# One sum and one product a chunk on GpSimd in 20 chunks, and newly ordered queues, in a gated linear recurrence followed by a gated convolution

## The chip, the cores and the metric

The kernel runs on one core of one Trainium2 chip. The metric is the time of one execution in microseconds (us); lower is better. The kernel before takes 281.59 us, the median of three runs.

## What is computed

The inputs x, r_gate and i_gate are float32 tensors of 4 sequences x 6336 steps x 256 channels. The reference, cut to what matters:

```python
# stage 1: gated linear recurrence along the sequence
a_base = 1 / (1 + exp(-a_param))                      # one number a channel
log_a  = 8 * sigmoid(r_gate) * log(clip(a_base, 1e-6, 1 - 1e-6))
a_t    = exp(log_a)
x_gated = sqrt(maximum(1 - a_t * a_t, 1e-6)) * sigmoid(i_gate) * x
h = 0
for t in range(S):                                    # S = 6336, per sequence
    h = a_t[:, t] * h + x_gated[:, t]
    y[:, t] = h
# stage 2, on y
gate = sigmoid(causal_conv(y, conv_w))                # 5 taps, channel by channel
out  = (gate * (y @ w_val)) @ w_out                   # both 256 x 256
```

## The kernel before

The four sequences are laid end to end: 25344 rows of 256 channels. They are cut into windows of 512 rows (window 49 has 256), and windows into 27 chunks: chunks 0, 1, 25 and 26 are one window each, chunks 2 to 24 are two, so that chunk c holds the windows 2c-2 and 2c-1. A window of r, i and x is loaded with rows on the partitions; the recurrence needs channels on the partitions, and TensorE transposes in between. The 256 channels are two halves, h = 0 and 1. For output, window 49 is cut in two parts of 128 rows, 49 and 50.

Nothing is scheduled by the compiler. A string, `ORDER`, lists some 960 words; each word emits one step, and each engine, and the one queue that starts all large DMAs (SyncE, SP), works through its own steps in the order of the string. What follows the @ in a word are PSUM banks. A word is a step name, the chunk or window, and sometimes the half. With the lines of the kernel before, the steps are:

- SP: `lr`, `li`, `lx` load a window of r, i, x (line 292) into rings of four windows (`rring`, `iring`, `xring`); `st` stores a window from `oring` (line 562); `s_wl` loads parts of the weights. A load waits until the earlier content of its place has been read, and everything behind it in the queue waits too.
- ACT (ScalarE): `ta`, `tb` tanh of r and i of a chunk (lines 310, 313); `ex` the decay a, by Exp, into `aring` (373; from chunk 2 to 23 two chunks at once); `rt` the square root of a batch of chunks (406, between two table loads at 578); `tg` tanh of the convolution of a window (518); `ca` copies a window's result to `oring` (551); `sa` squares the decay (389).
- POOL (GpSimd): `sq` squares the decay of a chunk's half into `ering` (381); `pp` adds 1 to the tanh of i of one window in place in `tbring` (320); `up` multiplies that by x into `uring` (332); `s_wcast` casts the weights.
- DVE (VectorE): `rd` a square root by arithmetic for chunk 0 (419 to 427, eight operations); `uv` the product of x in windows 0, 2, 4, 8 and 9, where TensorE has brought x to PSUM (346); `xg` times the root (452, and 456 from chunk 24 on); `sc` the scan along time (499); `gv` gate times value (531); `cd` copies a window's result to `oring` (549).
- PE (TensorE): `tr` (357), `xp` (337), `nt` (441) and `xt` (466) transposes, `cv` the convolution (511), `vl` the product with w_val (526), `ou` the product with w_out (541).

A chunk therefore runs: loads, `ta`, `tr`, `ex`, squares, `rt`, `nt`, then (with `tb`, `pp`, `up` beside it) `xg`, `xt`, `sc`; then by windows `cv`, `tg`, `vl`, `gv`, `ou`, `ca` or `cd`, `st`. The roots are taken in batches: chunk 0 by `rd.0.0`; chunk 1, and chunks 2 and 3, by `rt.1.0` and `rt.2.0`; then four chunks at a time by `rt.3` to `rt.7`, in two pieces each; chunk 24 by `rt.8.0`, chunks 25 and 26 by `rt.8.1`. From chunk 24 on `xg` follows the transpose, and the scan reads `uring` instead of PSUM.

Of the kernel before, what the change touches and what calls it, by code (L numbers as in the profile page):

```python
# [9 lines left out]
P = 128  # L10
CONV_K = 5
# [15 lines left out]
NU = 10  # L27
# [8 lines left out]
NOSB = 4  # L36
GROUPS = [[0], [1], [2, 3], [4, 5], [6, 7], [8, 9], [10, 11], [12, 13], [14, 15], [16, 17], [18, 19], [20, 21], [22,
# [7 lines left out]
s_ident s_small s_kt s_diag lr.1 lr.0 lr.2 lr.3 li.0 ta.1 lr.5 tr.1.1@3 ta.0 tr.1.0@1 ex.1.0 lr.4 tr.0.1@2 li.1 ex.0.1  # L45
tr.0.0@1 lx.0 ex.0.0 sq.0.1 ta.2 sq.0.0 sq.1.0 rd.0.0 tb.0 lr.6 lr.7 ex.1.1 li.3 li.2 sq.1.1 ta.3 lx.1 s_wl.0 lx.3 tb.1
tr.2.1@2,3 li.5 pp.1 ex.2.1 tr.2.0@0,1 s_wl.3 ex.2.0 lx.2 sq.2.1 lr.8 ta.4 sq.3.0 s_wl.1 tb.2 lr.9 xp.0@0,1 sq.3.1 li.4
uv.0 s_wl.2 nt.0@6 sq.2.0 xg.0 li.7 rt.1.0 li.6 xt.0.0@2 up.1 sc.0.0 rt.2.0 nt.1@0 lx.4 xt.0.1@3 sc.0.1 xp.2@6,7 pp.3
lx.5 xg.1 lr.11 uv.2 up.3 lr.10 nt.2@0,1 xt.1.0@2 ta.5 cv.0@4,5 sc.1.0 s_wcast xg.2 tb.3 lr.12 tr.4.1@2,3 lr.13
xt.1.1@6 xt.2.1@0 sc.1.1 tg.0 li.9 sc.2.1 li.8 ex.4.1 vl.0@4,5 xt.2.0@1 tr.4.0@6,7 tb.4 gv.0 sq.5.1 cv.1@2,3 sc.2.0  # L50
ex.4.0 li.11 pp.5 lx.7 xp.4@4,5 lx.6 pp.6 uv.4 ta.6 pp.7 nt.3@6,7 up.5 ou.0.0@0,1 ta.7 lr.14 cv.3@4,5 cd.0.0 li.10
sq.5.0 lx.9 xg.3 tg.3 cv.2@0,1 lr.15 tg.1 lx.8 st.0 vl.1@6,7 sq.4.1 tg.2 xt.3.1@4 gv.1 tb.5 tr.6.0@0,1 sc.3.1 up.7
tr.6.1@6,7 ex.6.0 vl.2@2,3 up.6 lx.11 gv.2 li.12 ou.1.0@4,5 ex.6.1 lr.17 cd.1.0 xt.3.0@2 lr.16 sq.4.0 lx.10 sc.3.0
li.13 tb.6 ou.2.0@6,7 sq.7.0 vl.3@0,1 ta.8 li.15 cv.4@4,5 gv.3 sq.6.1 cd.2.0 tg.4 lr.18 ou.3.0@2,3 cd.3.0 sq.7.1
xp.8@0,1 lx.12 uv.8 rt.3.0 li.14 vl.4@2,3 st.1 sq.6.0 gv.4 lr.19 xp.9@6,7 uv.9 pp.11 lx.13 ou.4.0@2,3 rt.3.1 pp.10
cd.4.0 st.2 nt.4@6,7 up.10 xg.4 nt.5@0,1 xg.5 xt.4.0@4 up.11 lx.14 sc.4.0 xt.5.0@3 nt.6@6,7 tb.7 xt.4.1@2 sc.4.1
# [553 lines left out]
```

## Time and profile before

| | before |
|---|---|
| runs | 281.40, 281.59, 281.83 us; median 281.59 |
| span of the profiled execution | 279.6 us from the first to the last instruction; the median of the runs is 2.0 us longer |
| busy: ACT, DVE, PE, POOL | 267.0, 258.2, 243.8, 233.0 us (96, 92, 87, 83% of the span) |
| granted TensorE clock, mean | 0.993 |
| DMA | 104.75 MB, mean 375 GB/s; 405 to 420 GB/s in most slices before 240 us |

The page is of one execution. Its second part shows how the engines' busy share moves through the span, in 40 slices of 7 us. In the lists of groups a duration is the mean of one instruction; on ACT, DVE and POOL an instruction starts about 0.05 to 0.15 us before the one ahead of it ends, so that from start to start is a little less than the duration. "Before" a group stands the idle time of its engine and what ended it.

### The profile page before, as it was taken

How to read it: one execution, taken by the hardware profiler on the slowest of the kernel's cores; microseconds unless marked ns; L12 is line 12 of the kernel's file. 1: busy time of each engine (PE TensorE's matmuls, PEld its weight loads, DVE VectorE, ACT ScalarE, POOL GpSimd, SP SyncE). 2: the span in 40 equal slices, each digit the busy share in tenths (PEclk: the TensorE clock that was granted, in tenths of full speed). 3: DMA queues.
4: the chain of work that ended last, by engine and by line, in shares of the span. 5: the costliest groups of instructions: out<-in, count | busy, mean ns of one | idle time of the engine just before them, and what ended most of it. 6: DMA issues, size and time to landing. Idle time of an engine off the chain costs nothing. (4 is left out here: it accounts for less than half of the span.)

```text
span 279.6 us, 6233 instructions
## 1 busy us (share of the span) xinstructions
PE 243.8 (87%) x2493; PEld 164.9 (59%) x2493; DVE 258.2 (92%) x221; ACT 267.0 (96%) x187; POOL 233.0 (83%) x152
## 2 busy tenths in 40 slices
PE   2368999898799779999889999899999899999994
PEld 2143566456647466874566575666675756856563
DVE  5587797899999999899999999999999999999992
ACT  5999999999999999999999999999999999999754
POOL 1569679997999998999999999999999977984200
PEclk9998899999999999999999999999999999999999
DMA  7999999999999999999999999999999999742765
GB/s 275 411 405 385 388 409 409 413 409 409 419 408 417 415 414 416 413 416 409 420 413 341 415 420 414 414 411 420 416 363 407 420 378 400 286 176 92 283 263 194
DMA packets 29563, 104.75 MB, mean 375 GB/s; under 512 B 3287, under 2 KB 4062, under 8 KB 29534
## 3 DMA queue, kind: packets, MB, share of 16 engines
q1 hardware_dynamic: 29520, 104.35, 94.4%
q8 instruction: 19, 0.31, 0.4%
q14 instruction: 10, 0.08, 0.1%
q10 hardware_dynamic: 14, 0.01, 0.0%
HBM read 78.39 MB, written 25.95 MB: 373 GB/s over the span
## 5 line engine op out<-in xcount | busy, mean ns | idle before, releaser
L381 POOL TENSOR_TENSOR ering<-aring 128x1024 f32<-128x1024 f32 (+1 forms) x51 | 90.7, 1799 | 13.8 <-ACT aring L373 13.7
L332 POOL TENSOR_TENSOR uring<-tbring,xring 128x1024 bf16<-128x1024 bf16 (+1 forms) x45 | 95.5, 2139 | 3.2 <-DMA xring<-in_x_dram 1.7
L499 DVE TENSOR_TENSOR_SCAN yring<-aring,yring,banks 128x1024 bf16<-128x1024 f32 (+4 forms) x46 | 96.8, 2116 | 0.8 <-PE banks L466 0.7
L511 PE MATMUL banks<-yring,diag 64*64 64x512 bf16 (+6 forms) x1080 | 63.1, 362 | 3.8 <-ACT aring L373 1.1
L531 DVE SCALAR_TENSOR_TENSOR tgring<-tgring,banks 128x1024 bf16<-128x1024 bf16 (+1 forms) x51 | 59.4, 1178 | 6.1 <-PE banks L526 5.1
L320 POOL TENSOR_SCALAR tbring<-tbring 128x1024 bf16<-128x1024 bf16 (+1 forms) x45 | 46.3, 1040 | 10.3 <-ACT tbring L313 10.3
L541 PE MATMUL banks<-wo,tgring 128*128 128x256 bf16 x396 | 50.9, 273 | 4.4 <-DVE tgring L531 2.1
L373 ACT ACTIVATE aring<-banks,khf 128x2048 f32<-128x2048 bf16 (+3 forms) x32 | 52.9, 1689 | 0.2 <-PE banks L357 0.2
L526 PE MATMUL banks<-yring,wv 128*128 128x512 bf16 (+4 forms) x216 | 50.1, 361 | 2.7 <-DVE oring L549 1.0
L518 ACT ACTIVATE tgring<-banks 128x1024 bf16<-128x1024 f32 (+1 forms) x51 | 50.6, 1011 | 0.8 <-PE banks L511 0.6
L541 PEld LDWEIGHTS <-tgring 128*128 128x128 bf16 x396 | 42.3, 114 | 14.2 <-DVE tgring L531 5.8
L310 ACT ACTIVATE taring<-rring 128x2048 bf16<-128x2048 f32 (+2 forms) x27 | 47.9, 1785 | 1.7 <-DMA rring<-in_r_gate_dram 1.7
L313 ACT ACTIVATE tbring<-iring 128x2048 bf16<-128x2048 f32 (+2 forms) x27 | 48.1, 1782 | 0.0
L511 PEld LDWEIGHTS <-diag 64*64 64x64 bf16 x1080 | 29.4, 105 | 27.7 <-issue 12.5
L406 ACT ACTIVATE ering<-ering 128x4096 bf16<-128x4096 f32 (+3 forms) x14 | 43.6, 3157 | 0.1
L549 DVE COPY oring<-banks 128x1024 f32<-128x1024 f32 (+1 forms) x34 | 39.9, 1189 | 0.4 <-PE banks L541 0.4
L357 PE MATMUL banks<-ident_b,taring 128*128 128x128 bf16 x396 | 29.4, 230 | 8.5 <-ACT taring L310 4.5
L466 PE MATMUL banks<-ident,uring 128*128 128x128 f32 x198 | 30.3, 279 | 4.4 <-DVE uring L452 1.6
L357 PEld LDWEIGHTS <-taring 128*128 128x128 bf16 x396 | 26.0, 103 | 12.3 <-issue 6.3
L526 PEld LDWEIGHTS <-wv 128*128 128x128 bf16 x216 | 19.1, 97 | 23.8 <-issue 10.2
L466 PEld LDWEIGHTS banks<-ident,uring 128*128 128x128 f32 x198 | 21.9, 141 | 14.5 <-DVE uring L452 3.4
L441 PEld LDWEIGHTS banks<-ident,ering 128*128 128x128 f32 x184 | 24.2, 208 | 6.8 <-issue 3.0
(52 smaller groups left out, 160.0 us busy)
## 6 DMA issues: line engine op xcount, KB each, us to landing
rring<-in_r_gate_dram SPq DMA_DIRECT2D x49, 512.0 KB, 8.4
iring<-in_i_gate_dram SPq DMA_DIRECT2D x49, 512.0 KB, 9.0
xring<-in_x_dram SPq DMA_DIRECT2D x49, 512.0 KB, 9.4
out_dram<-oring SPq DMA_DIRECT2D x49, 512.0 KB, 9.0
oring<-in_moe_w_val_dram SPq DMA_DIRECT2D x1, 256.0 KB, 8.9
rring<-in_r_gate_dram SPq DMA_DIRECT2D x1, 256.0 KB
iring<-in_i_gate_dram SPq DMA_DIRECT2D x1, 256.0 KB, 6.5
xring<-in_x_dram SPq DMA_DIRECT2D x1, 256.0 KB
```

The source lines that it names most:

```text
L313: nc.scalar.activation(**tangent(c, tbring, NTI, iring, NII))
L332: nc.gpsimd.tensor_tensor(out=u, in0=t1, in1=xt, op=ALU.mult)
L357: nc.tensor.transpose(out=bank[:, o:o + P], in_=taring[:, place(w, NTR), j, h * P:(h + 1) * P], identity=ident_b[:])
L373: nc.scalar.activation(out=dst, in_=src, func=ACT.Exp, scale=khf[:, h:h + 1], bias=khf[:, h:h + 1])
L381: nc.gpsimd.tensor_tensor(out=e, in0=a, in1=a, op=ALU.mult)
L466: nc.tensor.transpose(out=out[:, o + q:o + wins[w] // 2:nq], in_=uring[:, w % NU, q, h * P:(h + 1) * P, :].rearrange("p d two -> p (d two) ...
L499: nc.vector.tensor_tensor_scan(out=yring[:, h, col:col + o1 - o0], data0=aring[:, h, a_at[c] + o0:a_at[c] + o1], data1=xT[:, o0:o1], initi ...
L511: nc.tensor.matmul(out=gp[oh * 64:oh * 64 + 64, h, a:b], lhsT=diag[half * 64:half * 64 + 64, h, k, :], rhs=yring[half * 64:half * 64 + 64, ...
L518: nc.scalar.activation(out=tgring[:, w % NTG, :, 0:outs[w]], in_=live.pop(("gp", w))[:, :, 0:outs[w]], func=ACT.Tanh, scale=0.5)
L526: nc.tensor.matmul(out=val[:, m, a:b], lhsT=wv[:, hk, m * P:(m + 1) * P], rhs=yring[:, hk, col:col + b - a], start=(hk == 0), stop=(hk == ...
L531: nc.vector.scalar_tensor_tensor(out=tgring[:, w % NTG, :, 0:outs[w]], in0=tgring[:, w % NTG, :, 0:outs[w]], scalar=1.0, in1=live.pop(("va ...
L541: nc.tensor.matmul(out=ops[:, j * D:(j + 1) * D], lhsT=gv[:, hk, j:outs[w]:J], rhs=wo[:, hk, :], start=(hk == 0), stop=(hk == H - 1))
```

## The change

1. In 20 chunks (4 and 6 to 24) the two `pp` and the two `up` of a chunk become one `pq` and one `uq`, each over both windows: 40 sums and 40 products on GpSimd become 20 and 20. Windows 1, 3, 5, 48 and 49 keep `pp` and `up`, windows 0, 2, 4, 8 and 9 keep `uv`.
2. `ORDER` is written anew for all engines. Beside the order, six steps move to another engine: the squares `sq.0.1`, `sq.1.0`, `sq.1.1` go from GpSimd to ACT (`sa.0.1`, `sa.1.0`, `sa.1.1`); the squares `sa.21.1`, `sa.26.0`, `sa.26.1` go from ACT to GpSimd; the copy of window 28 goes from DVE (`cd`) to ACT (`ca`).
3. The set-up steps `s_kt` and `s_diag` are split, so that their parts on PE and DVE stand in the order by themselves; the set of instructions is the same.
4. `op_vl` may use one bank for a part of 128 rows (windows 49 and 50 do). New functions for loads and transposes by whole chunks are there, but `WHOLE` is empty and the order names none of them: transposes and loads go by windows as before.

The diff, cut to its core:

```diff
+WHOLE = ""
...
 ORDER = """
-s_ident s_small s_kt s_diag lr.1 lr.0 lr.2 lr.3 li.0 ta.1 lr.5 tr.1.1@3 ta.0 tr.1.0@1 ex.1.0 lr.4 tr.0.1@2 li.1 ex.0.1
...
+s_ident s_small lr.1 lr.0 lr.2 lr.3 s_ktp s_wl.2 s_ktd li.0 ta.1 s_dgp tr.1.0@0 tr.1.1@4 s_dgc ex.1.0 s_dgd ex.1.1
...
+        def whole(c, which):
+            return which in WHOLE and len(cwins[c]) == 2
...
+        def op_pq(c):
+            w, k = cwins[c][0], len(cwins[c])
+            t = tbring[:, place(w, NTI):place(w, NTI) + k, 0:wins[w] // P, :].rearrange("p k j d -> p (k j d)")
+            nc.gpsimd.tensor_scalar(out=t, in0=t, scalar1=1.0, scalar2=1.0, op0=ALU.mult, op1=ALU.add)
+
+        def op_uq(c):
+            w, k = cwins[c][0], len(cwins[c])
+            nc.gpsimd.tensor_tensor(
+                out=uring[:, w % NU:w % NU + k].rearrange("p k q d two -> p (k q) two d"),
+                in0=tbring[:, place(w, NTI):place(w, NTI) + k].rearrange("p k (q two) d -> p (k q) two d", two=2),
+                in1=xring[:, w % NX:w % NX + k].rearrange("p k (q two) d -> p (k q) two d", two=2), op=ALU.mult)
...
-        def op_vl(w, at, _):
-            val = banks[:, at:at + 2]
+        def op_vl(w, *at):
+            val = banks[:, at[0]:at[0] + 2] if len(at) == 2 else banks[:, at[0]].rearrange("p (h n) -> p h n", h=H)
+            assert len(at) == 2 or outs[w] <= 256
```

The first place is the start of ACT's queue. Before, up to the first pair of chunks (the last row is `ex.2.1` and `ex.2.0`); line 310 is `ta`, 313 `tb`, 373 `ex`:

```order
L310 ACTIVATE taring<-rring 128x1024 x2
L373 ACTIVATE aring<-banks,khf 128x512 x3
L310 ACTIVATE taring<-rring 128x2048
L313 ACTIVATE tbring<-iring 128x1024
L373 ACTIVATE aring<-banks,khf 128x512
L310 ACTIVATE taring<-rring 128x2048
L313 ACTIVATE tbring<-iring 128x1024
L373 ACTIVATE aring<-banks,khf 128x2048 x2
```

The same piece of ACT's queue in the changed kernel, where line 336 is `ta`, 339 `tb`, 412 `ex` and 434 `sa`:

```order
L336 ACTIVATE taring<-rring 128x1024
L412 ACTIVATE aring<-banks,khf 128x512 x2
L336 ACTIVATE taring<-rring 128x1024
L434 ACTIVATE ering<-aring 128x512 x2
L412 ACTIVATE aring<-banks,khf 128x512 x2
L336 ACTIVATE taring<-rring 128x2048
L339 ACTIVATE tbring<-iring 128x1024
L336 ACTIVATE taring<-rring 128x2048
L434 ACTIVATE ering<-aring 128x512
L339 ACTIVATE tbring<-iring 128x1024
L412 ACTIVATE aring<-banks,khf 128x2048 x2
```

Three squares have come in, the last of them (`sa.0.1`) behind `ta.3`, and the first Exp (`ex.1.0`) stands directly behind the first tanh (`ta.1`) instead of behind two.

The second place is the end of GpSimd's queue, from the products of chunk 23 on. Before; line 320 is `pp`, 332 `up`, 381 `sq` (of chunk 25 the 128x512 rows, of chunk 24 the 128x1024 rows):

```order
L332 TENSOR_TENSOR uring<-tbring,xring 128x2x2x256
L381 TENSOR_TENSOR ering<-aring 128x512
L381 TENSOR_TENSOR ering<-aring 128x1024
L381 TENSOR_TENSOR ering<-aring 128x512
L381 TENSOR_TENSOR ering<-aring 128x1024
L320 TENSOR_SCALAR tbring<-tbring 128x1024 x2
L332 TENSOR_TENSOR uring<-tbring,xring 128x2x2x256 x2
L320 TENSOR_SCALAR tbring<-tbring 128x1024
L332 TENSOR_TENSOR uring<-tbring,xring 128x2x2x256
```

In the changed kernel, where line 363 is `pq`, 367 `uq`, 420 `sq`, 346 `pp` and 358 `up` (128x256 are the squares of chunk 26):

```order
L367 TENSOR_TENSOR uring<-tbring,xring 128x4x2x256
L420 TENSOR_TENSOR ering<-aring 128x1024
L420 TENSOR_TENSOR ering<-aring 128x512
L363 TENSOR_SCALAR tbring<-tbring 128x2048
L367 TENSOR_TENSOR uring<-tbring,xring 128x4x2x256
L420 TENSOR_TENSOR ering<-aring 128x1024
L420 TENSOR_TENSOR ering<-aring 128x512
L420 TENSOR_TENSOR ering<-aring 128x256 x2
L346 TENSOR_SCALAR tbring<-tbring 128x1024
L358 TENSOR_TENSOR uring<-tbring,xring 128x2x2x256
```

Sum and product of chunk 24 now stand ahead of the second square of that chunk (`sq.24.0`), and the squares of chunk 26 have come in behind it.

193 lines of the change are left out of this document (109 added, 84 removed).

## The prediction

> **What bounds the kernel now.** I read the busy shares first, then the busy times by stretches, then the order of time on ACT and DVE at the two ends. The profiled execution spans 279.6 us and the median of the runs is 281.59 us; every sum below is made on the profile's clock, and the 2.0 us between the two are carried over unchanged.
>
> The first part of the page, then busy times in some stretches of the span (PE, PEld, DVE, ACT, POOL, the granted clock, the DMA share, GB/s):
>
> ```profile
> PE 243.8 (87%) x2493; PEld 164.9 (59%) x2493; DVE 258.2 (92%) x221; ACT 267.0 (96%) x187; POOL 233.0 (83%) x152
> 20.34:46.16 25.82, 23.30 (x183) 13.47 (x182) 19.64 (x20) 25.58 (x17) 21.63 (x17) 0.93 1.03 396
> 46.16:60.00 13.84, 11.55 (x100) 7.61 (x99) 12.93 (x10) 13.81 (x9) 13.77 (x8) 1.00 1.03 411
> 120.00:140.00 20.00, 18.24 (x196) 11.43 (x188) 19.98 (x14) 19.97 (x14) 20.00 (x13) 1.00 1.03 415
> 250.00:260.00 10.00, 9.81 (x104) 5.84 (x103) 10.00 (x9) 9.95 (x10) 5.45 (x5) 1.00 0.34 122
> 260.00:270.00 10.00, 10.00 (x102) 6.75 (x106) 9.57 (x10) 6.31 (x7) 1.11 (x1) 1.00 0.59 235
> ```
>
> ACT is the engine without a gap: 25.58 of 25.82 us, 19.97 of 20, 9.95 of 10, up to 260. DVE joins it from about 60 us (19.98 of 20 in the middle) but stands idle for 6.2 us between 20.3 and 46.2 and for 0.9 more up to 60, 7.1 in all. After 260 ACT has gaps, and PE (10.00 of 10) and DVE carry the end. GpSimd is full in the middle too, yet the end does not hang on it: after 260 it has 1.11 us of work. So a saving on GpSimd is worth only what it releases on ACT, DVE or PE. The DMA is full as well (share 1.03), but ACT hardly waits for it.
>
> **The merges.** Groups of GpSimd's operations by shape (mean ns behind the comma):
>
> ```profile
> L332 POOL TENSOR_TENSOR uring<-tbring,xring 128x1024 bf16<-128x1024 bf16 x44 | 94.3, 2161 | 2.8 <-DMA xring<-in_x_dram 1.3 <-PE banks L526 0.7
> L332 POOL TENSOR_TENSOR uring<-tbring,xring 128x512 bf16<-128x512 bf16 x1 | 1.2, 1180 | 0.4 <-DMA xring<-in_x_dram 0.4
> L320 POOL TENSOR_SCALAR tbring<-tbring 128x1024 bf16<-128x1024 bf16 x44 | 45.7, 1049 | 6.2 <-ACT tbring L313 6.2
> L320 POOL TENSOR_SCALAR tbring<-tbring 128x512 bf16<-128x512 bf16 x1 | 0.6, 620 | 4.1 <-ACT tbring L313 4.1
> L381 POOL TENSOR_TENSOR ering<-aring 128x1024 f32<-128x1024 f32 x45 | 84.6, 1900 | 6.2 <-ACT aring L373 6.1
> ```
>
> Twice the 512 size is 2360 and 1240 ns, the 1024 size 2161 and 1049: a merge saves 0.20 and 0.19 us, a `pq` should take 1.91 us and a `uq` 4.12. In 20 chunks that is 7.8 us of GpSimd. If a merge saved nothing they would take 2.10 and 4.32; the trace has no 128x2048 operation on GpSimd, so both ends stay. I take the saving, since half the size shows it, and count 0 of it on the end, because ACT, which GpSimd feeds, had no gap that this could close. What hides a failure of it is GpSimd's own idle time (4.2 us from 20.3 to 46.2, 4.5 us from 250 to 260). A merge also has a price: a `uq` needs both windows of x and frees both places only at its end, up to 2.2 us later for the first. The `xg` behind it uses both windows anyway.
>
> **The start.** ACT's first operations, the next to an Exp, and what they need from DVE, GpSimd and PE (start, length):
>
> ```profile
> 4.31 1.06 ACT L310 ACTIVATE taring<-rring 128x1024 bf16<-128x1024 f32 x1 [1.29 <-DMA rring<-in_r_gate_dram]
> 5.61 1.06 ACT L310 ACTIVATE taring<-rring 128x1024 bf16<-128x1024 f32 x1 [0.24 <-DMA rring<-in_r_gate_dram]
> 6.57 2.24 ACT L373 ACTIVATE aring<-banks,khf 128x512 f32<-128x512 bf16 x3
> 8.71 1.90 ACT L310 ACTIVATE taring<-rring 128x2048 bf16<-128x2048 f32 x1
> 10.50 1.05 ACT L313 ACTIVATE tbring<-iring 128x1024 bf16<-128x1024 f32 x1
> 11.45 0.77 ACT L373 ACTIVATE aring<-banks,khf 128x512 f32<-128x512 bf16 x1
> 12.11 1.91 ACT L310 ACTIVATE taring<-rring 128x2048 bf16<-128x2048 f32 x1
> 15.15 4.01 ACT L373 ACTIVATE aring<-banks,khf 128x2048 f32<-128x2048 bf16 x2 [0.18 <-PE banks L357]
> 33.56 1.00 ACT L518 ACTIVATE tgring<-banks 128x1024 bf16<-128x1024 f32 x1
> 5.61 0.17 DVE L248 TENSOR_SCALAR khf<-kcol 128x2 f32<-128x2 f32 x1
> 5.42 1.07 PE L357 MATMUL banks<-ident_b,taring 128*128 128x128 bf16 x8 [0.56 <-ACT taring L310]
> 10.30 1.23 DVE L419 TENSOR_SCALAR banks<-ering 128x1024 f32<-128x1024 f32 x1 [3.45 <-POOL ering L381]
> ```
>
> Before, ACT goes from `ta.1` at 4.31 to `ex.2.1` at 15.15, 10.84 us. Now, from start to start: `ta.1` to `ex.1.0` 1.59 (it waits for `khf`, done at 5.78, and the transposes of 5.42, so it starts near 5.9); four Exp at 0.68 (between the 0.71 and 0.66 of those above), 2.72; `ta.0` 0.96; `ta.2` and `ta.3` 1.80 each; `tb.0` and `tb.1` 0.95 each; and three 128x512 squares. The trace has squares on ACT of 128x256 and 128x1024, here with their neighbours:
>
> ```profile
> 247.92 0.43 ACT L389 ACTIVATE ering<-aring 128x256 f32<-128x256 f32 x1
> 248.23 1.04 ACT L518 ACTIVATE tgring<-banks 128x1024 bf16<-128x1024 f32 x1
> 249.13 0.44 ACT L389 ACTIVATE ering<-aring 128x256 f32<-128x256 f32 x1
> 249.59 1.28 ACT L578 ACT_TABLE_LOAD   x1
> 250.89 3.29 ACT L406 ACTIVATE ering<-ering 128x2048 bf16<-128x2048 f32 x2
> 198.97 1.11 ACT L389 ACTIVATE ering<-aring 128x1024 f32<-128x1024 f32 x1
> 199.92 1.05 ACT L551 COPY oring<-banks 128x1024 f32<-128x1024 f32 x1
> 200.81 1.09 ACT L518 ACTIVATE tgring<-banks 128x1024 bf16<-128x1024 f32 x1
> ```
>
> From start to start they are 0.31 and 0.95 us; between them by size, a 128x512 is 0.53 (bounds 0.31 and 0.95), three are 1.6. The sum is 12.36, so `ex.2.1` starts at 16.7: **ACT is 1.5 us late**, and nothing hides that, since ACT has no gap afterwards.
>
> What ACT loses later: `sa.21.1` -0.95 and the two squares of chunk 26 -0.31 and -0.46; it gains `ca.28` at 0.89 (199.92 to 200.81). That is -0.83. At `rt.8.0`, which stands at 250.89, ACT is then 1.5 - 0.8 = **0.7 us late**, with its small waits elsewhere as they were. Its waits from 20 to 250 come to about 0.5 (0.24 in the row from 20.34, some 0.03 in 20 us after it, as from 120 to 140) and, with some 0.1 of lost overlap at each of three, to an estimated 0.8; without them it would be about level.
>
> DVE starts `rd.0.0` 5.5 us later: not when GpSimd's two squares are done (10.30), but behind `sa.0.1`, which stands after `ta.3` at about 15.2 and ends near 15.85. `rd` is eight operations, 10.0 us, so DVE goes on to `uv.0` at 25.9 instead of 21.3. The cover is the idle time: from the end of `rd` (20.34) to the start of `gv.1` (46.16) DVE works 19.64 us of 25.82, so with no wait left it would be at `gv.1` by 25.9 + 19.6 = 45.5, before its time. What it needs from ACT comes in time: `tg.1` now follows `tg.0` (33.56 before, so 35.1) behind 0.90 of `tg.0`, 2.0 of an Exp and 1.8 of a tanh, and ends near 40.8. From then on DVE has one copy less, 1.13 us (254.33 to 255.46 below). So I count 0; the case that the cover fails is a rival.
>
> **The end.** DVE's roots and scans there, and GpSimd's last product:
>
> ```profile
> 253.19 1.22 DVE L456 TENSOR_TENSOR uring<-banks,ering 128x2048 bf16<-128x2048 bf16 x1
> 254.33 1.21 DVE L549 COPY oring<-banks 128x1024 f32<-128x1024 f32 x1
> 255.46 2.34 DVE L499 TENSOR_TENSOR_SCAN yring<-aring,yring,uring 128x1024 bf16<-128x1024 f32 x1
> 259.96 3.29 DVE L499 TENSOR_TENSOR_SCAN yring<-aring,yring,uring 128x1024 bf16<-128x1024 f32 x1
> 259.94 1.18 POOL L332 TENSOR_TENSOR uring<-tbring,xring 128x512 bf16<-128x512 bf16 x1 [0.37 <-DMA xring<-in_x_dram]
> 252.68 2.17 POOL L332 TENSOR_TENSOR uring<-tbring,xring 128x1024 bf16<-128x1024 bf16 x1
> 267.03 1.22 DVE L531 SCALAR_TENSOR_TENSOR tgring<-tgring,banks 128x1024 bf16<-128x1024 bf16 x1 [0.43 <-PE banks L526]
> ```
>
> `rt.8.0` is done near 252.8 and `xg.24` starts at 253.19: 0.4 us of ACT's 0.7 are slack there, 0.3 arrive. The steps behind `rt.8` are the same set on ACT and DVE. `gv.47` now has two scans ahead of it, so its 0.43 us wait goes, but PE, without a gap from 260 to 270, decides there: counted 0, up to -0.4 for the range.
>
> On GpSimd `pq.24` and `uq.24` stand ahead of `sq.24.0`, for which `rt.8.0` waits. From the end of `tb.24` that is 1.91 + 4.12 + 1.90 = 7.9 us; ACT needs about 8.1 from there to `rt.8.0` (six tanh and copies of windows at 0.90, `ex.26.0` 0.46, `tb.25` 0.95, the table load 1.28). 0.2 us is left; without the merges' saving it is short by 0.2.
>
> Sum: 279.6 + 0.7 - 0.4 = 279.9, or **281.9 us** beside the median of 281.59 (0.1% more).
>
> One row speaks of a port. Two scans of one shape, both from `aring` and `uring`, took 2.34 and 3.29 us; the second ran beside GpSimd's product at 259.94. The Trainium skill (GPSIMD Engine Reference, section 1, Specifications) says that GpSimd shares its SBUF interfaces with VectorE and contends with VectorE instructions that have two SBUF inputs. By that rule, the trace agrees: +0.95 for such a meeting. The scans of chunks 0 to 23 read PSUM and are not touched.
>
> **The rivals.**
> - *DVE's late start is not covered* (slower). Place: 16 to 60 us. DVE must win back 5.5 - 1.1 = 4.4 of the 7.1 us. For it: some of these gaps are waits for transposes that themselves wait for scans. Against it: the chain above. If half of the 7.1 is won back, DVE is 5.5 - 3.55 - 1.13 = 0.8 late at `xg.24`; if a quarter, 2.6. Between them 1.5, which swallows ACT's 0.3: 281.6 + 1.5 = 283.1 us. Chance 0.22.
> - *Two meetings at the end instead of one* (slower). The product of window 48 starts at 252.68 before, beside `xg.24` and a copy; now the squares of chunk 26 stand ahead and it can overlap `sc.24.0`, with that of window 49 still beside `sc.24.1`: 0.3 + 0.95, 282.8 us. It decides if that product starts over 0.6 us later, beside `xg.24`, than before: then (252.68 + 2.17 = 254.85) it reaches the scan at 255.46. Against it: the product of window 49 can come earlier. Chance 0.08.
> - *`rt.8.0` or another root waits for GpSimd* because a merged operation costs as much as two, or for x: 0.5 to 1 more than the forecast, 282.7 us. Chance 0.10.
> - *ACT's waits go and the end tightens* (faster): 0.8 less on ACT and 0.4 at `gv.47`, 280.7 us. For it: GpSimd has 7.8 us more room. Chance 0.25.
> - *The change does not do what it says*: the merged operations save nothing. GpSimd would be up to 0.4 us a chunk slower than I take it; where that tells is the third rival, and elsewhere its idle time hides it.
>
> **How the numbers follow.** About 0.2%, 0.56 us, is what a measurement here can tell from no change. The forecast, within it, has 0.35; faster 0.25; the three slower rivals 0.40. The range goes from 280.6, the faster rival with its bound, to 283.5, past the middle of the DVE case; its end at a quarter's cover, 281.6 + 2.6 = 284.2, is left out.
>
> **What would show it.** Right: a 128x2048 product of 4.1 us and sum of 1.9; `rd.0.0` near 15.9; `ex.2.1` near 16.7; DVE without idle time from 50; `rt.8.0` near 251.6 and `xg.24` right behind it. Wrong: `rt.8.0` before 250.5 or after 252.5; DVE idle beyond 60; a wait of ACT for GpSimd over 0.5 us; scans of chunk 24 both at 3 us.

## The result: 4.7 us slower, and the profile after

The changed kernel takes 286.31 us (median; 285.70 to 286.55) against 281.59: a ratio of 1.0167, 95% interval 1.0153 to 1.0182. The forecast was 281.9, within 280.6 to 283.5: wrong. The profiled execution spans 284.3 us, the median of the runs 2.0 more, as before, so spans can be set against each other.

Busy times of the changed kernel, then two of the stretches whose rows were shown of before (PE, PEld, DVE, ACT, POOL, clock, DMA share, GB/s), and the whole stretch from 20 to 250 us:

```profile
PE 240.7 (85%) x2467; PEld 162.7 (57%) x2493; DVE 256.7 (90%) x220; ACT 269.1 (95%) x188; POOL 227.0 (80%) x112
20.34:46.16 25.82, 20.56 (x155) 12.69 (x160) 24.54 (x24) 25.03 (x16) 20.68 (x15) 1.00 1.03 408
120.00:140.00 20.00, 18.71 (x201) 11.29 (x202) 19.89 (x15) 20.00 (x14) 19.92 (x10) 1.00 1.03 416
20.00:250.00 230.00, 203.98 (x2085) 139.41 (x2112) 221.92 (x174) 227.59 (x146) 211.27 (x95) 1.00 1.01 398
```

The same long stretch of before:

```profile
20.00:250.00 230.00, 210.58 (x2159) 142.86 (x2158) 221.33 (x173) 229.45 (x152) 217.69 (x135) 0.99 1.01 399
```

From 120 to 140 us ACT still has no gap. From 20.34 to 46.16 it stands idle for 0.79 us instead of 0.24, and in the 230 us for 2.41 instead of 0.55. Which of its groups wait, from 20 to 250 us in the changed kernel (behind the bar: busy us, mean ns | idle time ahead of the group, and what ended it):

```profile
L412 ACT ACTIVATE aring<-banks,khf 128x2048 f32<-128x2048 bf16 (+3 forms) x27 | 48.1, 1794 | 1.1 <-PE banks L397 1.1
L568 ACT ACTIVATE tgring<-banks 128x1024 bf16<-128x1024 f32 x41 | 41.6, 1026 | 0.6 <-PE banks L561 0.3
L602 ACT COPY oring<-banks 128x1024 f32<-128x1024 f32 x8 | 8.1, 1014 | 0.4 <-PE banks L592 0.4
```

In before the same three groups wait 0.0 in this stretch. They are what PE hands to ACT: the Exp wait for transposes (`tr`, line 397), the tanh for convolutions, the copies for the product with w_out. ACT's order of time at the start, and at the three longest of these waits:

```profile
4.50 1.06 ACT L336 ACTIVATE taring<-rring 128x1024 bf16<-128x1024 f32 x1 [1.48 <-DMA rring<-in_r_gate_dram]
...
15.45 0.63 ACT L434 ACTIVATE ering<-aring 128x512 f32<-128x512 f32 x1
15.97 1.05 ACT L339 ACTIVATE tbring<-iring 128x1024 bf16<-128x1024 f32 x1
16.92 2.06 ACT L412 ACTIVATE aring<-banks,khf 128x2048 f32<-128x2048 bf16 x1
...
43.52 2.06 ACT L412 ACTIVATE aring<-banks,khf 128x2048 f32<-128x2048 bf16 x1 [0.73 <-PE banks L397]
...
115.78 1.02 ACT L568 ACTIVATE tgring<-banks 128x1024 bf16<-128x1024 f32 x1 [0.32 <-PE banks L561]
...
118.96 2.07 ACT L412 ACTIVATE aring<-banks,khf 128x2048 f32<-128x2048 bf16 x1 [0.36 <-PE banks L397]
```

`ex.2.1` starts at 16.92 instead of 15.15 (+1.77). Then come `ex.4.0` at 43.52, `tg.14` at 115.78 and `ex.12.0` at 118.96. What PE waited for ahead of the first of them, and ahead of the other two:

```profile
39.32 1.96 PE L375 MATMUL banks<-xring,ident 128*128 128x512 f32 x4 [0.94 <-DMA xring<-in_x_dram]
...
113.90 0.63 PE L516 MATMUL banks<-ident,uring 128*128 128x128 f32 x4 [0.58 <-DVE tgring L582]
```

In PE's queue `tg.14` and `ex.12.0` stand behind transposes `xt.9`, and the first of these transposes needs a bank that is read by a `gv` of DVE. So ACT waits for PE there, and PE for a bank. Ahead of `ex.4.0` PE waited for a load of x (`xp.4`). In all, ACT has eight waits over 0.03 us from 20 to 250 us, 2.03 us together; before has one, of 0.18.

How late ACT is against before at the same step, from the order of time on ACT in each profile (the two experiments are told below):

| us late | `ex.2.1` | `rt.3.0` | `rt.4.0` | `rt.5.0` | `rt.6.0` | `rt.7.0` | `rt.8.0` | last copy |
|---|---|---|---|---|---|---|---|---|
| changed kernel | 1.77 | 2.38 | 2.51 | 3.40 | 3.75 | 3.25 | 4.38 | 4.61 |
| `new_start` | 2.42 | 2.63 | 2.53 | 2.52 | 2.49 | 2.51 | 2.51 | 2.47 |
| `new_rest` | 0.25 | 0.68 | 0.81 | 1.69 | 2.04 | 1.55 | 2.67 | 2.90 |

(At `rt.7.0` the changed order has one tanh of 0.95 us moved behind it, so 3.25 is 4.2 like for like.) Each row is of one execution, and equal steps come at different times in different executions: in `squares_26`, which is before up to 250 us, `ex.2.1` comes 0.90 later than in before, and at `rt.3.0` two kernels that are alike up to there are 2.25 us apart (`rest_pe_moved`).

DVE's first root and its `gv.1`, a wait behind `rt.3.0`, and then the root and scans of chunk 24, with GpSimd's products of windows 48 and 49:

```profile
16.18 1.23 DVE L464 TENSOR_SCALAR banks<-ering 128x1024 f32<-128x1024 f32 x1 [9.32 <-ACT ering L434]
46.46 1.22 DVE L582 SCALAR_TENSOR_TENSOR tgring<-tgring,banks 128x1024 bf16<-128x1024 bf16 x1
65.82 2.36 DVE L502 TENSOR_TENSOR uring<-banks,uring 128x2048 bf16<-128x2048 bf16 x2 [2.81 <-PE banks L491]
257.92 1.23 DVE L506 TENSOR_TENSOR uring<-banks,ering 128x2048 bf16<-128x2048 bf16 x1 [0.42 <-PE banks L516]
260.19 2.34 DVE L549 TENSOR_TENSOR_SCAN yring<-aring,yring,uring 128x1024 bf16<-128x1024 f32 x1
264.97 2.41 DVE L549 TENSOR_TENSOR_SCAN yring<-aring,yring,uring 128x1024 bf16<-128x1024 f32 x1
257.91 2.16 POOL L358 TENSOR_TENSOR uring<-tbring,xring 128x1024 bf16<-128x1024 bf16 x1
264.06 1.18 POOL L358 TENSOR_TENSOR uring<-tbring,xring 128x512 bf16<-128x512 bf16 x1
```

And the merged groups on GpSimd:

```profile
L367 POOL TENSOR_TENSOR uring<-tbring,xring 128x2048 bf16<-128x2048 bf16 x20 | 82.5, 4126 | 4.5 <-DMA xring<-in_x_dram 3.6
L363 POOL TENSOR_SCALAR tbring<-tbring 128x2048 bf16<-128x2048 bf16 x20 | 38.1, 1904 | 6.8 <-ACT tbring L339 6.8
```

By their durations the merges save what was expected of them, 0.19 to 0.20 us each, and the time does not follow.

### The profile page after: what moved, and what is told of

Read it like the earlier page. It is cut to its first block, busy times and chain, and to the rows that moved or that the text cites. A ratio compares the mean times of both kernels' runs of the same rounds, so it can differ in the third digit from the quotient of the medians.

```text
span 284.3 us, 6180 instructions
## 1 busy us (share of the span) xinstructions
PE 240.7 (85%) x2467; PEld 162.7 (57%) x2493; DVE 256.7 (90%) x220; ACT 269.1 (95%) x188; POOL 227.0 (80%) x112
## 4 chain that ended last, share of the span: by engine, by line
DMA 24%; PE 23%; ACT 19%; DVE 13%; POOL 10%; issue 8%; SPq 1%; DVEq 0%; ACTq 0%; POOLq 0%
DMA xring<-in_x_dram 10%; DMA rring<-in_r_gate_dram 7%; DVE yring L549 7%; DMA iring<-in_i_gate_dram 6%; PE banks L592 6%; PE banks L561 6%; PE banks L577 5%; POOL ering L420 4%; POOL uring L367 4%; ACT ering L451 4%; ACT aring L412 3%; DVE tgring L582 3%; ACT tgring L568 3%; ACT tbring L339 3%; ACT taring L336 3%
## 5 line engine op out<-in xcount | busy, mean ns | idle before, releaser
L420 POOL TENSOR_TENSOR ering<-aring 128x1024 f32<-128x1024 f32 (+2 forms) x51 | 90.3, 1797 | 15.2 <-ACT aring L412 15.1
L367 POOL TENSOR_TENSOR uring<-tbring,xring 128x2048 bf16<-128x2048 bf16 x20 | 82.5, 4126 | 4.5 <-DMA xring<-in_x_dram 3.6
L592 PEld LDWEIGHTS <-tgring 128*128 128x128 bf16 x396 | 41.7, 114 | 16.3 <-issue 6.7
L577 PE MATMUL banks<-yring,wv 128*128 128x512 bf16 (+6 forms) x190 | 47.9, 359 | 2.8 <-DVE uring L384 0.5
L561 PEld LDWEIGHTS <-diag 64*64 64x64 bf16 x1080 | 28.5, 105 | 27.5 <-issue 12.5
L363 POOL TENSOR_SCALAR tbring<-tbring 128x2048 bf16<-128x2048 bf16 x20 | 38.1, 1904 | 6.8 <-ACT tbring L339 6.8
L600 DVE COPY oring<-banks 128x1024 f32<-128x1024 f32 (+1 forms) x33 | 38.9, 1191 | 0.5 <-issue 0.2
L491 PE MATMUL banks<-ident,ering 128*128 128x128 f32 x184 | 26.6, 290 | 5.9 <-ACT ering L451 3.2
L502 DVE TENSOR_TENSOR uring<-banks,uring 128x2048 bf16<-128x2048 bf16 (+1 forms) x24 | 27.7, 1167 | 3.4 <-PE banks L491 3.3
```

The source lines that it names most:

```text
L367: nc.gpsimd.tensor_tensor(out=uring[:, w % NU:w % NU + k].rearrange("p k q d two -> p (k q) two d"), in0=tbring[:, place(w, NTI):place(w, ...
L420: nc.gpsimd.tensor_tensor(out=e, in0=a, in1=a, op=ALU.mult)
L561: nc.tensor.matmul(out=gp[oh * 64:oh * 64 + 64, h, a:b], lhsT=diag[half * 64:half * 64 + 64, h, k, :], rhs=yring[half * 64:half * 64 + 64, ...
L577: nc.tensor.matmul(out=val[:, m, a:b], lhsT=wv[:, hk, m * P:(m + 1) * P], rhs=yring[:, hk, col:col + b - a], start=(hk == 0), stop=(hk == ...
L592: nc.tensor.matmul(out=ops[:, j * D:(j + 1) * D], lhsT=gv[:, hk, j:outs[w]:J], rhs=wo[:, hk, :], start=(hk == 0), stop=(hk == H - 1))
```

## The experiments

Differences are against the runs of before on the same chip, and intervals are 95% intervals of the ratio. Line numbers of kernels made from the changed file differ from its own by up to three.

**The change in four parts.** At `xt.1.0` and `xt.1.1`, ahead of ACT's `tb.3`, both versions of the order have done much the same, so the two sides can be joined crosswise. In `new_start` the changed order runs up to there, before's order follows, and nothing is merged:

```diff
-s_ident s_small s_ktp s_ktd s_dgp s_dgc s_dgd lr.1 lr.0 lr.2 lr.3 li.0 ta.1 ... sq.0.1 ta.2 sq.0.0 sq.1.0 rd.0.0
+s_ident s_small lr.1 lr.0 lr.2 lr.3 s_ktp s_wl.2 s_ktd li.0 ta.1 ... sa.1.0 tr.0.0@0 lr.4 sa.1.1 ... lx.0 sa.0.1
```

> The changed order up to the transposes of xt.1.1 (about the first 35 us, with the three squares on ACT and the late root of chunk 0), then the order of before, without merged operations. If the start is the whole cause (what ACT and the load queue lose there is never won back), all 4.7 us show: near 286.3. If ACT's lateness alone carries through, 1.8 us: near 283.4. If the old order behind it has cover for it, under 0.6 us: 281.6 to 282.2.

Measured: 283.47 us, +1.9 (1.0047 to 1.0085). `ex.2.1`, `rt.8.0`, and then DVE's `xg.24`:

```profile
17.57 2.06 ACT L414 ACTIVATE aring<-banks,khf 128x2048 f32<-128x2048 bf16 x1
...
253.40 1.91 ACT L453 ACTIVATE ering<-ering 128x2048 bf16<-128x2048 f32 x1
255.70 1.22 DVE L508 TENSOR_TENSOR uring<-banks,ering 128x2048 bf16<-128x2048 bf16 x1
```

They are 2.42, 2.51 and 2.51 us later than before: what ACT loses in the first 17 us stands unchanged at 255. (This profile's `ex.2.1` is 0.65 later than the changed kernel's; its set-up steps finished later.)

`new_rest` is the other crossing: before's start, then the changed order with its merges.

```diff
-xt.1.0@2 ta.5 cv.0@4,5 sc.1.0 s_wcast xg.2 tb.3 lr.12 tr.4.1@2,3 lr.13 xt.1.1@6 xt.2.1@0 sc.1.1 tg.0
+xt.1.0@2 ta.5 cv.0@6,7 sc.1.0 s_wcast xg.2 tb.3 lr.12 tr.4.1@0,1 lr.13 xt.1.1@4 xt.2.0@2 lx.6 sc.1.1 lx.7 tg.0
```

> The reverse: the order of before up to xt.1.1, then the changed order with the merged operations. If the start is the whole cause: no more than 282.2. If the start is worth 1.8 us and the rest adds waits of its own: 284 to 284.8. If the start does not matter and the rest is the cause: near 286.3.

Measured: 284.74 us, +3.2 (1.0073 to 1.0160). The two halves, 1.9 and 3.2, make 5.1 beside the whole's 4.7: within their intervals they add up, so there are two causes. In this half ACT becomes late by steps (table above), though the changed order takes 0.83 us of work from it: between `ex.2.1` and `rt.8.0` it loses 2.67 - 0.25 + 0.83 = 3.25 us like for like, against 0.09 in `new_start`, where before's order stands behind the start.

`merges_undone` has the changed order, with each `pq` and `uq` replaced by the two operations of before:

```diff
-pq.4 ... uq.4
+pp.6 pp.7 ... up.6 up.7
```

> The changed order with each merged operation written as two again, side by side. If the merges are the cause: 2 us faster or more than the changed kernel, 284.3 and less. If they are a saving that this order needs (squares stand close ahead of the roots that wait for them): 1 to 3 us slower than it, 287.3 to 289. If they do not matter: 286.3 within 0.6.

Measured: 285.67 us, +4.1 (1.0097 to 1.0159). GpSimd has its work back, and the time is no longer for it; `rt.8.0` is at 255.39 beside 255.27. Its busy time is 232.6 us in all instead of 227.0: 5.6 us more, not the 7.8 that the durations gave, because an operation of GpSimd starts some 0.04 us before the one ahead of it ends, and durations count that time twice. So the merges do not help the changed order, and they are not what makes its 4.7 us. A small price is not excluded: the median is 0.64 below the changed kernel's (the intervals overlap), and in this profile ACT loses 2.04 us between `ex.2.1` and `rt.8.0` instead of 2.61.

`merges_only` puts the merges into before's order, each at the place of the later of the two steps:

```diff
-pp.11 ... pp.10 ... up.10 ... up.11
+pq.6 ... uq.6
```

> The order of before, with sum and product merged in the same 20 chunks, each at the place of the later of the two. If long products are the cause (squares and places of x wait behind them): 2 us slower or more, 283.6 and up. If a merge saves 0.39 us a chunk on an engine that ends nothing: within 0.6 us of 281.6.

Measured: 283.67 us, +2.1 (1.0046 to 1.0092): in before's order the merges cost time by themselves. In this profile `rt.8.0` is only 0.75 late, and the rest comes behind it; GpSimd's products of chunks 23 and 24, then `xg.24`:

```profile
238.09 4.13 POOL L367 TENSOR_TENSOR uring<-tbring,xring 128x2048 bf16<-128x2048 bf16 x1 [4.22 <-PE banks L516]
...
249.87 4.12 POOL L367 TENSOR_TENSOR uring<-tbring,xring 128x2048 bf16<-128x2048 bf16 x1
255.27 1.23 DVE L506 TENSOR_TENSOR uring<-banks,ering 128x2048 bf16<-128x2048 bf16 x1 [1.25 <-PE banks L516]
```

`uq.23` begins after 4.22 us of waiting, `uq.24` ends at 253.99, and `xg.24`, which needs its transposes, starts 1.28 later, 2.08 behind before. The trace names PE as the last releaser of `uq.23`. But the load of its second window of x, `lx.45`, took 7.3 us from its issue and landed at 237.84, only 0.25 us ahead of the start of `uq.23`. Its issue on SP:

```profile
230.51 0.42 SPq L299 DMA_DIRECT2D xring<-in_x_dram  x1
```

The same load in before:

```profile
227.81 0.46 SPq L292 DMA_DIRECT2D xring<-in_x_dram  x1
```

It went out 2.70 us later because of the load ahead of it in SP's queue, `lx.46`, which needs the place of window 42. In before `up.42` frees that place at 226.93, and `lx.46` goes out at 226.96; here `uq.22` frees it at 229.62, and `lx.46` goes out at 229.65. And where before's `up.44` starts at 232.81 with its own window, the whole of `uq.23` waits for the second one. So in this profile the late end is the price that the prediction named: both windows needed at once, and both places freed late.

**The merges again.** `merges_to_22` leaves the merges of chunks 23 and 24 out of `merges_only`:

```diff
-pq.23 ... uq.23 ... pq.24 ... uq.24
+pp.44 ... up.44 ... pp.45 ... up.45 ... pp.47 ... pp.46 ... up.47 ... up.46
```

> Before's order with the sums and products of chunks 4 and 6 to 22 merged at the place of the later one, and those of chunks 23 and 24 left as two each (merges_only, which merges these too, took 283.67 us). Theory (in before's order the merges cost most at the end, where one product of chunk 23 waits 4.2 us for the second window of x): the root rt.8.0 stays 0.75 us late by the small waits for merged products, and the end with it, 282.3 us. Rival (the price lies in the merged products throughout): as merges_only, 283.5 us.

Measured: 284.02 us, +2.5 (1.0059 to 1.0109). The theory falls: it is no faster than `merges_only`, although its words up to chunk 22 are the same. This time ACT is 3.01 late at `rt.8.0`. Two loads of x on SP, with the time that their issue took, and then the largest waits of ACT:

```profile
73.02 5.84 SPq L299 DMA_DIRECT2D xring<-in_x_dram  x2
81.14 1.02 ACT L568 ACTIVATE tgring<-banks 128x1024 bf16<-128x1024 f32 x1 [0.84 <-PE banks L561]
...
165.18 1.91 ACT L339 ACTIVATE tbring<-iring 128x2048 bf16<-128x2048 f32 x1 [0.62 <-DMA iring<-in_i_gate_dram]
```

The same two loads in before:

```profile
71.98 1.41 SPq L292 DMA_DIRECT2D xring<-in_x_dram  x2
```

Behind `rt.8.0` nothing is lost here (3.00 late at `xg.24`, 2.75 at the last copy). Whether the end's price has gone cannot be read from that: GpSimd's product of window 46 ends at 254.44, still 2.86 later than before, and ACT's own lateness covers it. Other prices came. A merged product frees both places of x only at its end, so SP stood for 5.84 us over two loads instead of 1.41 (5.70 in `merges_only`), with the loads of r and i behind them in the one queue; at 162.64 and 165.18 us two tanh wait 0.31 and 0.62 us for r and i. Why ACT had to wait at these places in this profile and not in the other stays open. What holds in both: in before's order the merged operations cost 2 to 2.5 us.

**The start.** `start_squares` is before with only the three squares on ACT, in their old places:

```diff
-sq.0.1 ... sq.1.0 ... sq.1.1
+sa.0.1 ... sa.1.0 ... sa.1.1
```

> The order of before, with nothing merged; only the three squares sq.0.1, sq.1.0 and sq.1.1 move from GpSimd to ACT in the places of the order where they stood (sa.0.1, sa.1.0, sa.1.1). DVE's rd.0.0 comes no later than before by it. Theory (every microsecond that ACT loses at the start arrives at the end, because no later place gives it back): ex.2.1 about 1.6 us later than before, the last copy of ACT 1.6 later, 283.2 us. Rival (ACT's lateness is won back from its small waits of 0.8 us): at most 0.8 later at the end, 282.4 us. Rival (the change's start cost what it did through DVE's late root and the loads, and ACT's squares are covered): within 0.3 of before, 281.6 us.

Measured: 282.85 us, +1.3 (1.0034 to 1.0067). `ex.2.1`, `rt.8.0`, and `xg.24`:

```profile
17.17 2.06 ACT L414 ACTIVATE aring<-banks,khf 128x2048 f32<-128x2048 bf16 x1 [0.18 <-PE banks L399]
252.49 1.91 ACT L453 ACTIVATE ering<-ering 128x2048 bf16<-128x2048 f32 x1
254.79 1.22 DVE L508 TENSOR_TENSOR uring<-banks,ering 128x2048 bf16<-128x2048 bf16 x1
```

`rt.8.0` and `xg.24` are 1.60 late, both of them, as much as three squares of 0.53 are worth from start to start. That is the theory's result, but its number is met in part by luck: `ex.2.1` is 2.02 late, 0.27 of it by a load of r ahead of the squares, and 0.3 is won back by 44 us, where before's `ta.7` waits 0.18 us for a load and this one does not. So most of what ACT loses at the start arrives, not all. There is no slack between `rt.8.0` and `xg.24`.

`late_root` moves only one square to ACT and DVE's root with it:

```diff
-sq.0.1 ta.2 sq.0.0 sq.1.0 rd.0.0 tb.0 lr.6 lr.7 ex.1.1 li.3 li.2 sq.1.1 ta.3
+ta.2 sq.0.0 sq.1.0 tb.0 lr.6 lr.7 ex.1.1 li.3 li.2 sq.1.1 ta.3 sa.0.1 rd.0.0
```

> The order of before, with nothing merged; only the square sq.0.1 moves from GpSimd to ACT and stands behind ta.3, with rd.0.0 behind it, as in the changed kernel. So ACT has 0.53 us more at the start and DVE's root of chunk 0 comes some 4 to 5 us later. Theory (DVE's idle time from 20 to 60 us covers its late root): no more than ACT's 0.53 arrives, 282.1 us, and gv.1 starts within 0.5 us of where it did. Rival (the cover fails, as the first rival of the prediction had it): DVE 1.5 us or more late at 60 us, 283.1 us or more.

Measured: 282.30 us, +0.8 (1.0022 to 1.0053). DVE's root, `gv.1`, and ACT at 45 us:

```profile
14.61 1.23 DVE L466 TENSOR_SCALAR banks<-ering 128x1024 f32<-128x1024 f32 x1 [7.78 <-ACT ering L436]
...
47.38 1.22 DVE L584 SCALAR_TENSOR_TENSOR tgring<-tgring,banks 128x1024 bf16<-128x1024 bf16 x1 [1.28 <-PE banks L579]
44.97 2.86 ACT L570 ACTIVATE tgring<-banks 128x1024 bf16<-128x1024 f32 x3 [0.78 <-DVE oring L602]
```

The root is 4.3 us late and DVE has idle time left at `gv.1`, so its lateness is mostly covered, and the rival's 1.5 us did not come. But `gv.1` started 1.2 later, not within 0.5, and one wait of 0.78 has arisen on ACT, which the trace puts down to a copy of DVE (PE's convolutions beside it start at 43.64 instead of 42.42). This wait makes the 0.8, not the square: right ahead of it, at `ta.7` (42.28), ACT is 0.03 late, because before's small waits at `ex.2.1` and `ta.7`, 0.18 each, are gone and have taken up the 0.53; at `rt.3.0` it is 0.91 late. So DVE's late root does reach ACT, with about half of what the rival had.

**What ACT waits for.** `rest_pe_moved` is `new_rest` with two steps moved on PE:

```diff
-xg.10 xt.9.1@4 ex.12.1 li.25 pq.11 cv.14@0,1 ... cd.12.0 xt.9.0@1 tr.12.0@4,5
+xg.10 cv.14@0,1 xt.9.1@4 ex.12.1 li.25 pq.11 ... cd.12.0 tr.12.0@4,5 xt.9.0@1
```

> The kernel with before's start and the changed order behind it (new_rest, 284.74 us), with two steps of PE moved: the convolution cv.14 goes ahead of the transposes xt.9.1, and the transposes tr.12.0 ahead of xt.9.0, so that tg.14 and ex.12.0 no longer wait on ACT behind transposes whose bank is not free yet (waits of 0.32 and 0.36 us, near 0.45 each with the lost overlap). Theory (each such wait of ACT behind PE's order arrives at the end, since ACT has no room to win it back): 0.9 us less than new_rest, 283.8 us, and ACT about 2.0 late at the end instead of 2.9. Rival (another limit, PE, DVE or the loads, sets ACT's lateness and the waits move to other places): 284.5 to 284.9 us, and new waits of ACT between 110 and 140 us.

Measured: 285.64 us, +4.1 (1.0123 to 1.0180); no gain over `new_rest`, whose interval overlaps. ACT at `tg.14`, `ex.12.0` and `tg.15`:

```profile
115.88 1.03 ACT L568 ACTIVATE tgring<-banks 128x1024 bf16<-128x1024 f32 x1
...
119.18 2.07 ACT L412 ACTIVATE aring<-banks,khf 128x2048 f32<-128x2048 bf16 x1 [0.47 <-DVE oring L600]
...
125.04 1.02 ACT L568 ACTIVATE tgring<-banks 128x1024 bf16<-128x1024 f32 x1 [0.19 <-PE banks L561]
```

The wait at `tg.14` is gone, the one at `ex.12.0` has grown from 0.36 to 0.47 and is now ended by DVE, and a new one stands at `tg.15`. From `rt.4.0` to `rt.5.0` ACT loses 0.88 us, exactly as in `new_rest`. So the rival holds: the waits move. (ACT was already 2.25 us behind `new_rest` at `rt.3.0` in this profile, ahead of the place that was edited; that is not the edit's doing.)

Three kernels then take work from one resource at a time and keep the changed order. `light_dve`:

```diff
+            n = 256 if 4 <= w < 40 else outs[w]
-            nc.vector.scalar_tensor_tensor(out=tgring[:, w % NTG, :, 0:outs[w]],
+            nc.vector.scalar_tensor_tensor(out=tgring[:, w % NTG, :, 0:n],
```

> The changed kernel, but the gate times value (gv) of windows 4 to 39 is formed for 256 of 512 steps only, so the other half of the result of these windows is not what the reference has. It takes some 0.55 us from DVE in each of 36 windows, 20 us in all before 250 us, and leaves the order and everything behind window 39 as it is. ACT's idle time and lost overlap from 20 to 240 us come to 4.5 us in the changed kernel and to 1.7 in the kernel before. Theory (behind ACT's waits for PE stands DVE, which frees PE's banks late): most of the 2.8 us goes, rt.8.0 starts 2 to 3 us sooner than in the changed kernel, 283.5 to 284.3 us. Rival (PE's own work or the loads are what ACT waits for): less than 1 us sooner, 285.4 us or more.

`light_pe`:

```diff
+            taps = 3 if 4 <= w < 40 else CONV_K
-                for k in range(CONV_K):
+                for k in range(taps):
```

> The changed kernel, but the convolution (cv) of windows 4 to 39 has 3 of its 5 taps, so the results of these windows are not what the reference has. It takes 8 of 20 products from each, an estimated 0.5 us of PE's time by window (58.6 us in 920 products), some 17 us in all before 250 us, and leaves the order and everything behind window 39 as it is. Theory (behind ACT's waits for PE stands DVE): less than 1 us sooner than the changed kernel, 285.4 us or more. Rival (PE's amount of work is what ACT waits for): rt.8.0 2 to 3 us sooner, 283.5 to 284.3 us.

`light_dma`:

```diff
+            if which == "i" and 8 <= w < 44:
+                dst, src = dst[:, 0:J // 2, :], src[:, 0:J // 2, :]
```

> The changed kernel, but of the input i of windows 8 to 43 only half the rows are loaded, the other half of the place keeping rows of an earlier window, so that results from window 8 on are not what the reference has. It takes 9.4 of 104.8 MB from the transfers, some 23 us at 405 GB/s, and leaves the order as it is. Theory (behind ACT's waits stand DVE and PE): less than 1 us sooner than the changed kernel, 285.4 us or more. Rival (the transfers, which are full all the way, are behind it): rt.8.0 2 to 3 us sooner, 283.5 to 284.3 us.

Measured: 283.92 us (1.0052 to 1.0097), 284.32 (1.0064 to 1.0161) and 285.73 (1.0121 to 1.0152), against the changed kernel's 286.31. Busy times from 20 to 250 us, first of `light_dve`:

```profile
20.00:250.00 230.00, 207.01 (x2150) 140.86 (x2151) 208.68 (x175) 229.46 (x150) 213.62 (x95) 1.00 1.00 399
```

of `light_pe`, with the one group of ACT that waits there:

```profile
20.00:250.00 230.00, 194.53 (x1832) 131.55 (x1836) 223.72 (x175) 228.52 (x149) 212.22 (x95) 1.00 1.00 399
L339 ACT ACTIVATE tbring<-iring 128x2048 bf16<-128x2048 f32 (+1 forms) x24 | 45.2, 1892 | 1.0 <-DMA iring<-in_i_gate_dram 1.0
```

and of `light_dma`:

```profile
20.00:250.00 230.00, 206.12 (x2116) 140.18 (x2120) 222.01 (x174) 227.71 (x147) 211.35 (x95) 0.99 0.96 356
```

The first column behind the clock shows the transfers: only in `light_dma` do they fall under full, 0.96 and 356 GB/s, and ACT's idle time stays at 2.29 us. With DVE relieved it is 0.54, before's value, and `rt.8.0` comes at 252.15, 3.12 sooner. With PE relieved it is 1.48, of which 1.0 is one wait for a load late in the stretch.

Not all of this is the edits' doing. They begin with window 4, shortly ahead of `rt.3.0` (in `light_dma` with window 8), and the wait at `ex.4.0` stands ahead of them: it is 0.51 in `light_dma` and missing in `light_dve` and `light_pe`, and also in `merges_undone`, so it comes and goes with the execution. What the edits do is read from `rt.3.0` on:

| us late against before | `ex.2.1` | `rt.3.0` | `rt.7.0` | from `rt.3.0` to `rt.7.0` |
|---|---|---|---|---|
| changed kernel | 1.77 | 2.38 | 3.25 | +0.87 |
| `light_dve` | 1.63 | 1.33 | 0.47 | -0.86 |
| `light_pe` | 1.69 | 1.70 | 0.59 | -1.11 |
| `light_dma` | 1.56 | 2.06 | 2.92 | +0.86 |

Between these two roots the changed order has 1.01 us less work on ACT (a square of 0.95 gone, a tanh of 0.95 moved behind, a copy of 0.89 more), so about -1.0 means that nothing is lost. That is so with DVE relieved and with PE relieved; with fewer bytes of i nothing changes. The medians say the same, 2.4, 2.0 and 0.6 us below the changed kernel's (the profile of `light_dve` is of one of its faster executions, 282.94). So both texts were half right: it is neither engine alone, either will do. Fewer bytes do not help, though `light_dma` leaves the loads of x as they are and the transfers 0.96 busy. In the changed order PE's and DVE's steps come just too late for ACT at several places, at `tg.14` and `ex.12.0` by way of a PSUM bank, and either one's room takes the waits behind `rt.3.0` away. Which moved step makes which wait stays open.

**The other direction.** `squares_26` is before with ACT's two squares of chunk 26 on GpSimd, which could have been faster than both kernels:

```diff
-up.47 tb.25 ... sa.26.1 up.46 tg.41 vl.40@0,1 sa.26.0
+up.47 sq.26.1 sq.26.0 tb.25 ... up.46 tg.41 vl.40@0,1
```

> The kernel before with one thing changed: the two squares of chunk 26 (128x256) go from ACT to GpSimd, behind the product of window 47. So ACT has 0.77 us less ahead of rt.8.0, while the product of window 48 comes some 1.1 us later and reaches over the first scan of chunk 24 (255.46 in before). Theory (every microsecond of ACT's work ahead of rt.8.0 counts, in this direction as well): rt.8.0 0.77 sooner, 280.8 us. Rival (the prediction's slack at xg.24): 0.4 of it is slack, 281.2 us. Rival (the meeting of that product with the first scan, which takes 3.3 us then instead of 2.34): 281.6 to 282.2 us.

Measured: 282.06 us, +0.4 (0.9998 to 1.0027): not told apart from before. `rt.8.0`, GpSimd's product of window 46, then on DVE `xg.24` and the second scan of chunk 24, and GpSimd's product of window 49:

```profile
250.81 3.29 ACT L406 ACTIVATE ering<-ering 128x2048 bf16<-128x2048 f32 x2
251.84 2.16 POOL L332 TENSOR_TENSOR uring<-tbring,xring 128x1024 bf16<-128x1024 bf16 x1
255.29 1.22 DVE L456 TENSOR_TENSOR uring<-banks,ering 128x2048 bf16<-128x2048 bf16 x1 [1.48 <-PE banks L466]
...
262.06 2.99 DVE L499 TENSOR_TENSOR_SCAN yring<-aring,yring,uring 128x1024 bf16<-128x1024 f32 x1
261.74 1.17 POOL L332 TENSOR_TENSOR uring<-tbring,xring 128x512 bf16<-128x512 bf16 x1 [0.42 <-DMA xring<-in_x_dram]
```

ACT did win: 0.54 late at `tb.25`, 0.08 early at `rt.8.0`. But the product of window 46 now ends at 254.00 instead of 251.58, and `xg.24`, whose transposes need it, waits 1.48. None of the three texts had this. The profile is of the slowest of ten executions (283.35), and GpSimd was 1.28 late in it ahead of the two squares; the squares account for the other 1.14. So the median's 0.4 and no gain fit a price on GpSimd that eats ACT's 0.6, but its usual size was not seen. None of the kernels tried was faster than before.

## Why the prediction was wrong, by its own steps

*The merges* were right: 1.904 and 4.126 us for forecasts of 1.91 and 4.12, and nothing gained at the end. The 7.8 us of GpSimd's time were too many: its busy time fell by 5.6 (`merges_undone`). That the merges cost nothing either holds in the changed order only, and there up to some 0.6 us. In before's order the price the step named, both windows of x needed at once and both freed late, shows on SP (5.84 us for 1.41) and makes the late end of `merges_only`, though no run isolates its part of the 2 us.

*ACT's start* was right in kind and nearly in size: three squares at 0.53 each (15.45 to 15.97 is 0.52), `ex.2.1` at 16.92 for a forecast of 16.7. It was 1.77 late, not 1.5; 0.19 of that is the first load of r, which let `ta.1` start at 4.50 instead of 4.31. That nothing hides it is nearly right: `new_start` brings all of its 2.42 us to `rt.8.0`, `start_squares` 1.60 of 2.02. ACT had small gaps, and in `late_root` two of them swallow a whole square.

*The step that failed* is "0.7 us late, with its small waits elsewhere as they were". `rt.8.0` came at 255.27, 4.38 late. The terms of work hold: 1.77 - 0.83 = 0.94, and with DVE relieved the changed order does come at 1.26. The remaining 3.4 are lost between `ex.2.1` and `rt.8.0`: eight new waits, 2.0 us together, and the rest in overlap lost at them and in small delays that the trace puts down to nothing single. The prediction put the waits at an estimated 0.8 that could only go; the changed order has more. It read ACT's queue and GpSimd's word for word and took over what PE, DVE and the loads hand to ACT. `new_rest` shows that the changed order behind the start makes these losses (3.25 us), and `light_dve` and `light_pe` that most of them behind `rt.3.0` hang on PE and DVE; the longest, 0.73 at `ex.4.0`, hung on a load of x in this execution. Its faster rival, in which GpSimd's room removes ACT's waits, falls with `merges_undone`.

*DVE's cover* held in the main: `rd.0.0` at 16.18 (forecast 15.9), `gv.1` at 46.46 without a wait, against 46.16. `late_root` shows that it is not free: the late root costs ACT a wait of 0.78, and the end 0.8. The rival had the mechanism in part, with a price of 1.5 that was twice too high, and the 2.81 us that DVE idles at 65.82 is not a failing cover but a wait for ACT's late root.

*The end.* The 0.4 us of slack at `xg.24` was not there: in `start_squares` and `new_start` the lateness of `rt.8.0` arrives at `xg.24` in full (1.60 and 1.60, 2.51 and 2.51). DVE's queue ahead of it had only moved with ACT. *`rt.8.0` waiting for GpSimd* did not happen. *Two meetings at the end* did not happen either; there was hardly one: the scans took 2.34 and 2.41 us, since GpSimd's product of window 49 ended at 265.24, 0.27 into the second scan. That gave back 0.9 of before's 3.29, which no term of the sum had, but PE and DVE turned it into nothing: the last copy is 4.61 late behind an `xg.24` that is 4.72 late.

## What to carry to other kernels

When ACT is full for 230 us, most of what is put into its first 17 us stands in the end time (2.02 late there and 1.60 at `rt.8.0`, 2.42 and 2.51), whereas the room made on an engine that it does not wait for is worth nothing. When a whole order is rewritten, sum the work per engine, but then ask for each engine's order what its neighbours hand it and when: eight waits of 0.04 to 0.73 us, with the overlap lost around them, cost more here than all moved work (3.4 us against 0.94), and they cannot be read from one queue. To find what stands behind such waits, take work from one engine at a time: the waits of ACT went with DVE's or PE's relief, and stayed with fewer bytes; moving single steps only moved them. But compare from a step behind which the edit acts: one of the waits that went had stood ahead of it.

## What the runs showed of the hardware

A scan from SBUF that starts while GpSimd runs a product is longer by the overlap less 0.2 us. Before, 259.96 to 261.12 is 1.16 us of overlap, and the scan took 3.29 us instead of 2.34 (+0.95). In `squares_26`, 262.06 to 262.91 is 0.85, and it took 2.99 (+0.65). In the changed kernel 0.27 of overlap gave 2.41 (+0.07). The product, which had started first, took its 1.17 to 1.18 us each time. In `merges_to_22` it was the other way round: the scan started first, by 0.02 us, took its 2.34, and the product grew from 1.18 to 3.30, by 2.12 for an overlap of 2.33:

```profile
262.96 2.34 DVE L549 TENSOR_TENSOR_SCAN yring<-aring,yring,uring 128x1024 bf16<-128x1024 f32 x1
262.98 3.30 POOL L358 TENSOR_TENSOR uring<-tbring,xring 128x512 bf16<-128x512 bf16 x1 [0.40 <-DMA xring<-in_x_dram]
```

What is added is the overlap less the same 0.2 us each time, not a share of it: the later of the two does not go slower, it stands still. The Trainium skill (SBUF — State Buffer, SBUF: two separate sides) says so: of a VectorE instruction with two SBUF inputs and a GpSimd instruction that reads SBUF, the one that starts first locks the ports that the two engines share, for its whole length, and the other is blocked. The traces agree up to the 0.2 us.

By their durations, one operation of GpSimd over twice the size is about 0.2 us shorter than two: 2 x 2.161 - 4.126 = 0.20 for products and 2 x 1.049 - 1.904 = 0.19 for sums. On the clock it is less, because two in a row overlap a little: before, two products at 247.33 take 4.25 us from the first start to the last end, 0.12 more than the merged one.
